# A fused linear-attention and snake-MLP kernel on one core: states of head pairs as one block-diagonal tile, transposes by two routes, a re-planned order of loads and weights, and lent PSUM banks

## The chip, the cores and the metric

One Trainium2 chip, one of its cores. The metric is the device time of one execution in microseconds (us), lower is better. The executions of one kernel mostly lie within one and a half per cent of their median here; those more than 1.5% above the fastest are called slow, and medians below are of fast runs. Each execution also has a *span*, from its first to its last instruction, which lies about 1.7 us under the time of that same execution (250.8 and 252.5 us for the profiled run of the kernel before). Engines: PE multiplies matrices, PEld loads its weights, DVE and POOL do elementwise work, ACT does table functions (exp, ln, sin) and copies, SP issues most of the DMA transfers. PSUM is the memory that PE writes to, used here in eight banks; SBUF is the large on-chip memory. The granted clock is the share of PE's full speed that it was allowed. The DMA share adds up the time of packets, so that it can go above 1.

## The reference, cut to what matters

```python
f = 1 / (1 + exp(-f_logit))                       # batch 4, heads 8, 768 steps, head size 48
for t in range(768):
    state = f[:, :, t, :, None] * state + einsum('bhd,bhe->bhde', k[:, :, t], v[:, :, t])
    y[:, :, t] = einsum('bhd,bhde->bhe', q[:, :, t], state)
x = y as (3072 tokens, 384)
h = x @ w_in                                      # 384 x 2048, "layer one"
g = h + sin(alpha * h)**2 / (alpha + 1e-9)
out = g @ w_out                                   # 2048 x 384, "layer two"
```

## The kernel before

The 768 steps are cut into 6 chunks of 128. Within a chunk, attention is done by matmuls: cumulated logs of the gates (tile cs), gated k and q (tile qk), their transposes (tp in PSUM, tr in SBUF), scores (aps), masked scores (at), output y, and the state (kv in PSUM, st in SBUF) which passes to the next chunk. Four batches make one chunk of 512 tokens (tile xT; in all chunks but the first, six small DMAs, the *spread*, move parts of it to other partitions); then layer one (tile h, 16 tiles of three 512-column matmuls), the sine s, its square, g, and layer two (tile o).

What is special is who decides the order. The kernel contains a small planner. Every operation is put in a list with estimated durations, the engines that may do it and the buffers that it takes; the planner simulates this and fixes one static order for each engine, with a few hand-tuned constants. On the chip each engine runs its list strictly in order.

```python
LAG = 50
ATT = 12
PHASES = [("pre", [0]), ("sin", 1), ("pre", [1, 2]), ("sin", 21), ...]   # ACT's order: exponentials or sines
def in_order(ops, lines):
    ...
            for e, dur in o.engs.items():
                s = max(t, free[e])
                ...
                key = (s + (BIAS[e] if len(o.engs) > 1 else 0), o.rank, s + d)
                if best is None or key < best[0]:
                    best = (key, o, e, s, d)
```

The transposes of chunk 0 are done on PE, those of chunks 1 to 5 by a transposing DMA on SP's queue; the states of two heads are kept as two 64-row halves:

```python
        def tr_(e):
            if e == SP:
                nc.sync.dma_start_transpose(t, qk_b[qkb.place % NQ].rearrange("c x p r e -> c (x p r e)"))
                return
            (nc.scalar.copy if e == ACT else nc.vector.tensor_copy)(t, tl[x, "tp"])
        def inter_(e):
            for p in range(HP):
                for r in range(2):
                    nc.tensor.matmul(y[halves[r], POS[p], :], tl["st", c - 1, b][halves[r], p, :],
                                     tl[x, "tr"][halves[r], HP + p, :], ...)
        ...
    for u in range(2, 2 * NCH):       # loads strictly in the order f, k, q, v of each pair of batches
        for n in "fkqv":
            load(u, n, EARLY + 10 + u)
```

Of the kernel before, what the change touches and what calls it, by code (L numbers as in the profile page):

```python
# [16 lines left out]
N_H, N_A, NQ, NV, NG = 3, 3, 6, 4, 22  # L17
LAG = 50
ATT = 12
PHASES = [("pre", [0]), ("sin", 1), ("pre", [1, 2]), ("sin", 21), ("pre", [3]), ("sin", 4), ("pre", [4]),  # L20
          ("sin", 6), ("pre", [5, 6]), ("sin", 15), ("pre", [7]), ("sin", 15), ("pre", [8, 9]), ("sin",
          6), ("pre", [10, 11]), ("sin", 44)]
RANK = [-100, 26, -206, 68, -82, 12, -28, -12, 36, 24, 32, 16]
MULS = {"POOL": 1180, "DVE": 1000}
BIAS = {"ACT": 300, "DVE": 100, "POOL": -800}
# [22 lines left out]
TABLE_LOAD, DMA_LATENCY, DMA_AHEAD = 1280, 1900, 3000  # L48


def in_order(ops, lines):


    free = dict.fromkeys(("PE", "ACT", "DVE", "POOL", "SP"), 2500)
    free["ACT"] = free["SP"] = 800
    dma_free, table = dict.fromkeys(("SP", "POOL"), 0), None
    follows = {}
    for o in ops:
        for d in set(o.deps):
            follows.setdefault(d, []).append(o)  # L60
    missing = {o: len(set(o.deps)) for o in ops}
    done, turn, nth = [], {o: i for x in lines.values() for i, o in enumerate(x)}, dict.fromkeys(lines, 0)

    def when(o):

        t = max([o.after] + [d.end + (LATENCY[d.eng] if d.eng not in o.engs or len(o.engs) > 1 or d.eng != "PE" else 0)
                             for d in o.deps])
        for b in o.takes:
            if b.place is None:
                i = len(b.ring.taken)  # L70
                if i >= b.ring.n:
                    old = b.ring.taken[i - b.ring.n]
                    if any(x.end is None for x in old.users):
                        return None
                    t = max([t] + [x.end + LATENCY[x.eng] for x in old.users])
        return t

    pending = [o for o in ops if not missing[o]]
    left = len(ops)
    while left:  # L80
        best = None
        for o in pending:
            if o.line and turn[o] != nth[o.line]:
                continue
            t = when(o)
            if t is None:
                continue
            for e, dur in o.engs.items():
                s = max(t, free[e])
                if o.dma:  # L90
                    s = max(s, dma_free[e] - DMA_AHEAD)
                d = dur + (TABLE_LOAD if o.table and o.table != table and table else 0)
# [3 lines that stand above are left out]
        if best is None:  # L96
            raise RuntimeError("no operation can start")
        _, o, e, s, d = best
        o.start, o.eng, free[e] = s, e, s + d
        o.end = s + d  # L100
        if o.dma:
            dma_free[e] = max(s + 600, dma_free[e]) + o.dma
            o.end = dma_free[e] + DMA_LATENCY
        table = o.table or table
        if o.line:
            nth[o.line] += 1
        for b in o.takes:
            if b.place is None:
                b.place = len(b.ring.taken)
                b.ring.taken.append(b)  # L110
        pending.remove(o)
        for x in follows.get(o, ()):
            missing[x] -= 1
            if not missing[x]:
                pending.append(x)
        done.append((o, e))
        left -= 1
    return done
# [3 lines left out]
def kernel(  # L122
# [58 lines left out]
    act_order, load_order, h_order = [], [], []  # L181

    def op(rank, engs, emit, deps=(), takes=(), holds=(), table=None, dma=None):
        o = Op(rank, engs, emit, [d for d in deps if d is not None], list(takes), table, dma)
        for b in list(takes) + list(holds):
# [23 lines left out]
                            pattern=[[-1, C]], channel_multiplier=1)  # L209
    ident_f = consts.tile([FB, FB], F32)  # L210
# [23 lines left out]
    def load(u, n, rank):  # L234
# [7 lines left out]
        o = bufs[n, u].ready = op(rank, {SP: 500}, emit, takes=[bufs[n, u]], dma=2500 if u < 2 else 2200)  # L242
# [11 lines left out]
    def w_in_load(hf, rank):  # L254
        for j, p0, r0, n in ((0, 0, 0, E), (1, 0, 80, E), (2, 16, 3 * D, D), (2, 0, D + 16, 16)):
            for r in range(2):
                def emit(e, j=j, p0=p0, r0=r0, n=n, r=r):
                    nc.gpsimd.dma_start(out=w_in_bf[r * E + p0:r * E + p0 + n, j, HF[hf]],
                                        in_=moe_w_in[4 * D * r + r0:4 * D * r + r0 + n, HF[hf]])
                w_in_dma[hf].append(op(rank, {POOL: 1000}, emit, dma=1300 if n == E else 1000 if n == D else 500))  # L260

    def w_out_load(rank):
        src = moe_w_out.rearrange("(fb p) m -> p fb m", p=P)
        for g4 in range(4):
            def emit(e, gs=slice(4 * g4, 4 * g4 + 4)):
                nc.gpsimd.dma_start(out=w_out_bf[:, gs, :], in_=src[:, gs, :])
            w_out_dma[g4] = op(rank + 0.1 * g4, {POOL: 1000}, emit, dma=3500)

    def alpha(rank):
# [11 lines left out]
        t.after = 6000  # L281
# [5 lines left out]
    def pre(u, rank):  # L287
# [26 lines left out]
        for i in range(2):  # L314
# [23 lines left out]
            def gl_(e, m=m):  # L338
                tl["gl", m] = at_pool.tile([P, HP], F32, tag="gl", bufs=6, name=f"gl_{m}")
                nc.vector.tensor_copy(tl["gl", m], tl["cs", m][:, H * D:H * D + HP])  # L340
# [6 lines left out]
            c_ = op(rank + i, {PE: 170 if last else 420}, cs_, deps=[l], takes=[cb], holds=[lf])  # L347
            gi = op(rank, {ACT: 450}, Gi_, deps=[c_], takes=[Gib], holds=[cb], table=EXP)
# [6 lines left out]
            if not last:  # L355
                made["gl", m] = op(rank + i, {DVE: 100}, gl_, deps=[g], takes=[glb], holds=[cb])
        return act, late

    def pres(us, rank):
        parts = [pre(u, r) for u, r in zip(us, rank)]  # L360
        for a, _ in parts:
            act_order.extend(a)
        for _, l in parts:
            act_order.extend(l)


    def attend(c, b, rank):
# [3 lines left out]
        tpb, trb, ab, atb = first and buf("a"), buf("tr"), [buf("a"), buf("a")], [buf("at0"), buf("at1")]  # L371
# [21 lines left out]
        def a_(e):  # L393
            t = tl[x, "tr"]
            aps = tl[x, "a"] = [ps_a.tile([P, HP, C], F32, tag="a", name=f"aps_{c}_{b}_{r}") for r in range(2)]
# [4 lines left out]
        def m_(e, r):  # L400
            a = tl[x, "at", r] = at_pool.tile([P, HP, C], BF16, tag=f"at{r}", name=f"at_{c}_{b}_{r}")
            nc.vector.tensor_mul(a, tl[x, "a"][r], mask4)  # L402

        def inter_(e):
            y = tl[x, "y"] = ps_a.tile([P, HP, C], F32, tag="a", name=f"y_{c}_{b}")
            for p in range(HP):
                for r in range(2):
                    nc.tensor.matmul(y[halves[r], POS[p], :], tl["st", c - 1, b][halves[r], p, :],
                                     tl[x, "tr"][halves[r], HP + p, :],
                                     start=(p == 0), stop=False, skip_group_check=True)  # L410
# [21 lines left out]
        def kv_(e):  # L432
            kv = tl[x, "kv"] = ps_a.tile([P, HP, E], F32, tag="a", name=f"kv_{c}_{b}")
            if not first:
                nc.tensor.matmul(kv, ident, tl["st", c - 1, b], start=True, stop=False, skip_group_check=True)
            for p in range(HP):
                for r in range(2):
                    nc.tensor.matmul(kv[halves[r], p, :], qk_b[qkb.place % NQ][:, 0, p, r, :], v_b[vb.place % NV][:, i, r, p, :],
                                     start=(first and p == 0), stop=True, skip_group_check=True)

        def st_(e):
            t = tl["st", c, b] = st_pool.tile([P, HP, E], BF16, tag=f"s{b}", name=f"st_{c}_{b}")
            nc.vector.tensor_tensor(t, tl[x, "kv"], tl["gl", m].unsqueeze(2).to_broadcast([P, HP, E]),
                                    Alu.mult)

        if first:
# [3 lines left out]
        else:  # L450
            tr = op(rank, {SP: 1300}, tr_, deps=[made["kh", m], made["qh", m]], takes=[trb], holds=[qkb], dma=1000)
        a = op(rank, {PE: 450}, a_, deps=[tr], takes=ab, holds=[trb])
        ms = [op(rank, {DVE: 690}, lambda e, r=r: m_(e, r), deps=[a], takes=[atb[r]], holds=[ab[r]]) for r in range(2)]
        last_ = None
        if not first:
            last_ = op(rank, {PE: 480}, inter_, deps=[a, made["st", c - 1, b]], takes=[yb], holds=[trb, sold])
# [5 lines left out]
        if not last:  # L462
            kv = op(rank + 1, {PE: 450}, kv_, deps=[made["kh", m], made["v", u], made.get(("st", c - 1, b))],
                    takes=[kvb], holds=[qkb, vb] + ([sold] if sold else []))
            made["st", c, b] = op(rank + 1, {DVE: 420}, st_, deps=[kv, made["gl", m]], takes=[sb], holds=[kvb, bufs["gl", m]])
# [13 lines left out]
    def first(c, fb, ts, rank, needs):  # L479
        n = ts.stop - ts.start  # L480
        half = n < TOK
        hb, sb, s2b = buf("h"), buf("s"), buf("s2")
# [4 lines left out]
        def mm(e):  # L487
            h = tl[x, "h"] = ps_h.tile([P, TOK], F32, tag="h", name=f"h_{c}_{fb}_{ts.start}")
# [24 lines left out]
        a.line = "h"  # L513
        h_order.append(a)
# [5 lines left out]
    def second(c, t, rank):  # L520
        ob, sbuf = buf("o"), buf("osb")
        prev = None
        for fb in range(FB):
# [6 lines left out]
            prev = op(rank + 0.5 * fb, {PE: 163}, mm, deps=[prev, g, w_out_dma[fb // 4]],  # L530
# [9 lines left out]
        op(rank, {SP: 500}, store, deps=[v_], holds=[sbuf], dma=500)  # L540
# [7 lines left out]
    for u in range(2):  # L548
        for n in "fkqv":
            load(u, n, EARLY)  # L550
# [3 lines left out]
    for u in range(2, 2 * NCH):  # L554
        for n in "fkqv":
            load(u, n, EARLY + 10 + u)
# [3 lines left out]
    for what, arg in PHASES:  # L560
        if what == "pre":
            pres(arg, [RANK[u] for u in arg])
            for u in arg:
                c = u // NU
                for b in (2 * (u % NU), 2 * (u % NU) + 1):
                    attend(c, b, base(c) - ATT + 4 * b)
                if u % NU and c:
                    spread(c, base(c) - ATT)
# [13 lines left out]
    for c in range(NCH):  # L582
        for t in range(B):
            second(c, t, base(c) + LAG + 4 * t)
# [3 lines left out]
    for o, e in in_order(ops, {"table": act_order, "load": load_order, "h": h_order}):  # L588
# [34 lines left out]
```

## Time and profile before

| | before |
|---|---|
| time | 254.7 us, median of 3 runs (254.52 to 257.35) |
| span of the profiled run | 250.8 us (that run took 252.5 us) |
| hardware DMA queue (loads, stores, transposes) | 69.3% of 16 engines |

From the page of the kernel before: busy time of each engine with its share of the span, the DMA queue that SP feeds (packets, MB, share of 16 engines), and one of the costlier groups (busy us, mean ns of one | idle time ahead of them, and what ended it):

```profile
PE 198.4 (79%) x1577; PEld 109.8 (44%) x1593; DVE 155.3 (62%) x306; ACT 140.3 (56%) x219; POOL 139.6 (56%) x168
...
q1 hardware_dynamic: 124608, 29.34, 69.3%
...
L398 PE MATMUL aps<-tr 64*128 64x128 bf16 x192 | 12.9, 249 | 7.7 <-DMA tr<-qk 2.6
```

PE is the busiest, but only 79%; the transposing DMAs (tr) hold PE's score matmuls for 2.6 us in all. Next the state's operations, from the groups of all instructions:

```profile
L408 PE MATMUL y<-tr,st 64*64 64x128 bf16 x160 | 9.1, 240 | 0.3 <-DVE st L443 0.3
L438 PE MATMUL kv<-vb,qk 128*64 128x64 bf16 x160 | 7.4, 212 | 1.7 <-POOL qk L343 1.7
L408 PEld LDWEIGHTS <-st 64*64 64x64 bf16 x160 | 5.7, 116 | 5.4 <-issue 4.7 <-DVE qk L343 0.2
L435 PE MATMUL kv<-st,ident 128*128 128x256 bf16 x16 | 4.6, 288 | 1.0 <-DVE qk L343 0.9
L383 PE MATMUL tp<-ident,qk 128*128 128x128 bf16 x32 | 4.1, 309 | 5.4 <-DVE qk L343 3.7 <-POOL qk L343 1.7
L443 DVE TENSOR_TENSOR st<-kv,gl 128x256 bf16<-128x256 f32 x20 | 8.2, 418 | 2.4 <-PE kv L438 2.3
```

The prediction's working rests on these and on the slices, stretches and waits that it shows itself.

### The profile page before, as it was taken

The page shows a single profiled execution, that of the slowest core. Times are in us where ns is not written, and L with a number is a line of the kernel's source. Part 1 is how long each engine was busy: PE and PEld are TensorE (multiplying, and loading weights), DVE is VectorE, ACT ScalarE, POOL GpSimd, SP SyncE. Part 2 cuts the span into 40 slices and gives each one's busy share as a digit, 9 for nine tenths or more (in the row PEclk, how much of TensorE's full clock was granted, in tenths as well). Part 3 has the DMA queues.
Part 4 walks back from the last instruction along what each step waited for, and adds up shares of the span by engine and source line. Part 5 has one row for each costly group of instructions (what it writes and reads, how often), then busy time and mean ns, then how long its engine had stood idle before and what let it go on. Part 6 is the DMA issues. An engine that isn't in the chain of part 4 may idle for free.

```text
span 250.8 us, 4495 instructions
## 1 busy us (share of the span) xinstructions
PE 198.4 (79%) x1577; PEld 109.8 (44%) x1593; DVE 155.3 (62%) x306; ACT 140.3 (56%) x219; POOL 139.6 (56%) x168
## 2 busy tenths in 40 slices
PE   0257107998688594999869999899999899999993
PEld 0145004565355351454434545455444345555552
DVE  3183106776384768497775784597797756666741
ACT  4307129345866487465765558969755454555500
POOL 8653007556342426468444754683758756788810
PEclk9999999999958677699977999999999999999999
DMA  8999999999999996999659802897640001100021
GB/s 140 188 195 207 188 202 187 171 188 196 177 178 183 218 157 107 228 176 189 118 104 191 122 4 66 158 168 169 147 97 5 31 3 68 42 33 34 31 95 63
DMA packets 127798, 32.77 MB, mean 131 GB/s; under 512 B 121392, under 2 KB 127008, under 8 KB 127776
## 3 DMA queue, kind: packets, MB, share of 16 engines
q1 hardware_dynamic: 124608, 29.34, 69.3%
q0 software_dynamic: 3168, 3.16, 8.0%
q8 instruction: 12, 0.20, 0.3%
q14 instruction: 10, 0.08, 0.1%
HBM read 25.17 MB, written 4.72 MB: 119 GB/s over the span
## 4 chain that ended last, share of the span: by engine, by line
PE 35%; POOL 18%; issue 15%; SPq 10%; DMA 9%; DVE 7%; ACT 4%; POOLq 0%; ACTq 0%; DVEq 0%
POOL s L504 16%; PE o L527 16%; PE h L491 14%; SPq L240 9%; DMA f<-in_f_logit_dram 5%; DMA v<-in_v_dram 3%; DVE g L509 2%; PE y L422 2%; POOL qk L343 2%; DVE at L402 2%; PE aps L398 1%; ACT Gi L336 1%; SPq L473 1%; ACT L591 1%; DVE osb L535 1%
## 5 line engine op out<-in xcount | busy, mean ns | idle before, releaser
L504 POOL TENSOR_TENSOR s<-s 128x512 f32<-128x512 f32 (+1 forms) x112 | 102.1, 923 | 58.5 <-ACT s L496 54.1
L496 ACT ACTIVATE s<-h,al_p 128x512 f32<-128x512 f32 (+1 forms) x112 | 68.7, 626 | 60.2 <-PE h L491 54.7
L509 DVE SCALAR_TENSOR_TENSOR g<-s,al_r,h 128x512 bf16<-128x512 f32 (+1 forms) x112 | 74.0, 668 | 30.5 <-POOL s L504 28.8
L491 PE MATMUL h<-xT,w_in_bf 128*128 128x512 bf16 (+1 forms) x320 | 84.6, 374 | 9.1 <-DVE g L509 4.2
L527 PE MATMUL o<-w_out_bf,g 128*128 128x384 bf16 x384 | 82.2, 334 | 0.1
L491 PEld LDWEIGHTS <-w_in_bf 128*128 128x128 bf16 x336 | 33.1, 103 | 37.9 <-issue 12.7
L527 PEld LDWEIGHTS <-g 128*128 128x128 bf16 x384 | 36.7, 99 | 28.2 <-issue 1.1
L343 POOL TENSOR_TENSOR qk<-k,Gi 128x384 bf16<-128x384 f32 x24 | 23.5, 1005 | 39.4 <-ACT Gi L336 39.3
L402 DVE TENSOR_TENSOR at<-aps,mask 128x512 bf16<-128x512 f32 x48 | 31.4, 684 | 8.2 <-PE aps L398 8.0
L323 PE MATMUL cs<-lf,mask 128*128 128x384 bf16 x24 | 8.4, 366 | 14.9 <-ACT lf L296 12.9
L422 PE MATMUL y<-at,vb 128*64 128x128 bf16 x184 | 18.9, 239 | 1.1 <-DVE at L402 0.7
L591 ACT ACT_TABLE_LOAD x15 | 19.2, 1283 | 0.3
L398 PE MATMUL aps<-tr 64*128 64x128 bf16 x192 | 12.9, 249 | 7.7 <-DMA tr<-qk 2.6
L293 ACT ACTIVATE f<-f 128x768 f32<-128x768 f32 x12 | 10.1, 839 | 13.1 <-DMA f<-in_f_logit_dram 13.0
L429 ACT CAST xT<-y 128x512 bf16<-128x512 f32 (+1 forms) x13 | 7.4, 567 | 17.3 <-PE y L422 17.3
L422 PEld LDWEIGHTS <-vb 128*64 128x64 bf16 x184 | 12.3, 119 | 10.3 <-issue 9.3
L340 DVE COPY gl<-cs 128x4 f32<-128x4 f32 x20 | 3.2, 159 | 21.3 <-ACT cs L332 21.3
L535 DVE COPY osb<-o 128x384 f32<-128x384 f32 x19 | 10.5, 556 | 9.0 <-PE o L527 8.7
L343 DVE TENSOR_TENSOR qk<-q,cs 128x384 bf16<-128x384 f32 x24 | 12.9, 546 | 2.9 <-DMA q<-in_q_dram 2.9
L336 ACT ACTIVATE Gi<-cs 128x384 f32<-128x384 f32 x24 | 11.6, 484 | 4.8 <-PE cs L326 4.5
L398 PEld LDWEIGHTS <-tr 64*128 64x128 bf16 x192 | 7.0, 105 | 14.6 <-issue 8.2
L326 PEld LDWEIGHTS <-lf 128*128 128x128 bf16 x80 | 5.0, 102 | 16.3 <-issue 15.1
(48 smaller groups left out, 129.3 us busy)
## 6 DMA issues: line engine op xcount, KB each, us to landing
f<-in_f_logit_dram SPq DMA_DIRECT2D x12, 384.0 KB, 6.5
k<-in_k_dram SPq DMA_DIRECT2D x12, 384.0 KB, 6.2
q<-in_q_dram SPq DMA_DIRECT2D x12, 384.0 KB, 7.2
v<-in_v_dram SPq DMA_DIRECT2D x12, 384.0 KB, 6.7
out_dram<-osb SPq DMA_DIRECT2D x24, 192.0 KB, 2.1
w_out_bf<-in_moe_w_out_dram POOLq DMA_DIRECT2D x4, 384.0 KB, 6.9
w_in_bf<-in_moe_w_in_dram POOLq DMA_DIRECT2D x8, 128.0 KB, 5.8
xT<-xT SPq DMA_DIRECT2D x30, 16.0 KB, 1.8
```

What stands on the lines that cost most here:

```text
L240: engine[e].dma_start(out=t, in_=srcs[n][bp * 2 * H:(bp + 1) * 2 * H, c * C:(c + 1) * C, :] .rearrange("b c d -> c b d"))
L336: nc.scalar.activation(out=tl["Gi", m], in_=tl["cs", m][:, :H * D], func=Act.Exp)
L343: engine[e].tensor_mul(qk_b[bufs["qk", m].place % NQ][:, "kq".index(n), :, :, :D], tl[n, u][:, i * H:(i + 1) * H, :].rearrange("c (r p) d ...
L398: nc.tensor.matmul(aps[r][:, p, :], t[halves[r], p, :], t[halves[r], HP + p, :], start=True, stop=True)
L402: nc.vector.tensor_mul(a, tl[x, "a"][r], mask4)
L422: nc.tensor.matmul(tl[x, "y"][halves[r], blk, :], v_, tl[x, "at", r][:, p, :], start=(first and p == 0), stop=True, skip_group_check=True)
L491: nc.tensor.matmul(h[:, :n], w_in_bf[:, kb, fs], xT[:, kb, ts], start=(kb == 0), stop=(kb == KB - 1))
L496: nc.scalar.activation(out=s[:, :n], in_=tl[x, "h"][:, :n], func=Act.Sin, scale=al_p[:, fb:fb + 1])
L504: engine[e].tensor_mul(s2[:, :n], s[:, :n], s[:, :n])
L509: nc.vector.scalar_tensor_tensor(tl["g", c, fb][:, ts], tl[x, "s2"][:, :n], al_r[:, fb:fb + 1], tl[x, "h"][:, :n], Alu.mult, Alu.add)
L527: nc.tensor.matmul(tl["o", c, t], tl["g", c, fb][:, t * P:(t + 1) * P], w_out_bf[:, fb, :], start=(fb == 0), stop=(fb == FB - 1))
L591: nc.scalar.preload_act_table_set(now)
```

## The change

The intent: fewer and wider state matmuls (a pair of heads as one 128 by 128 block-diagonal tile, half of it zero), fewer transposing DMAs in the stretch where DMA is full, an order of loads, weights and phases fitted to that, and two PSUM banks of layer two lent to layer one while layer two has nothing to do. The diff, cut to its core (left out are other constants of the planner, RANK, BIAS and the DMA latencies among them, which also change the order):

```diff
-N_H, N_A, NQ, NV, NG = 3, 3, 6, 4, 22
-LAG = 50
-ATT = 12
-PHASES = [("pre", [0]), ("sin", 1), ("pre", [1, 2]), ("sin", 21), ...]
+NG = 36
+PE_TR = 4
+SPARE = 25
+LOADS = [("f", 0), ("f", 1), ("k", 0), ("q", 0), ("v", 0), ("q", 1), ("v", 1), ("k", 1), ("f", 2), ...]
+W_AFTER = [15000, 22000, 52000]
+LAG = [50, 24, 32, 29, 28, 94]
+ATT = [-32, 18, 8, 12, -4, 16]
+PHASES = [("pre", [0]), ("pre", [1]), ("sin", 6), ("pre", [2]), ("sin", 16), ("pre", [3]), ("sin", 9), ...]
@@ the planner: weights now also count against SP's queue
+            if e == "POOL":
+                dma_free["SP"] = max(s + 600, dma_free["SP"]) + o.dma
@@ weights are not planned before a given time
+                o.after = W_AFTER[hf]
@@ transposes: chunks 0 to 3 on PE, 4 and 5 by DMA
-        if first:
+        if c < PE_TR:
@@ the state
-                for r in range(2):
-                    nc.tensor.matmul(y[halves[r], POS[p], :], tl["st", c - 1, b][halves[r], p, :],
-                                     tl[x, "tr"][halves[r], HP + p, :], ...)
+                nc.tensor.matmul(y[:, POS[p], :], tl["st", c - 1, b][:, p, :, :].rearrange("d r e -> d (r e)"),
+                                 tl[x, "tr"][:, HP + p, :], ...)
-            t = tl["st", c, b] = st_pool.tile([P, HP, E], BF16, ...)
+            t = tl["st", c, b] = st_pool.tile([P, HP, 2, E], BF16, ...)     # times gl, which is 0 off the diagonal
@@ lent banks
+        spare = c == 0 and nth < SPARE and nth % 5 > 2
-        hb, sb, s2b = buf("h"), buf("s"), buf("s2")
+        hb, sb, s2b = buf("o" if spare else "h"), buf("s"), buf("s2")
```

## The prediction

> **What bounds the kernel now.** I read the slices of the page first, then three long stretches of the span, then the same stretches for layer one alone (tile h), then the list of waits and the chain that ended last.
>
> ```profile
> PE   0257107998688594999869999899999899999993
> PEclk9999999999958677699977999999999999999999
> DMA  8999999999999996999659802897640001100021
> ```
>
> DMA is full for the first half of the span and almost idle in the last quarter; PE is the reverse. So there are two regimes. The stretches size them (columns: length, then busy us and count of PE, PEld, DVE, ACT, POOL; granted clock, DMA share, GB/s), first all work, then layer one alone (PE, DVE, ACT):
>
> ```profile
> 0.00:40.00 40.00, 12.79 (x117) 8.36 (x117) 12.94 (x47) 14.02 (x21) 17.69 (x37) 1.00 1.15 186
> 40.00:100.00 60.00, 46.97 (x435) 29.29 (x436) 41.52 (x95) 40.20 (x69) 29.47 (x43) 0.86 1.22 176
> 100.00:240.00 140.00, 131.56 (x985) 68.23 (x1000) 98.12 (x161) 86.05 (x130) 92.42 (x90) 0.96 0.53 100
> ...
> 0.00:40.00 40.00, 2.88 (x12) 0.48 (x1) 0.47 (x1) 1.00 1.15 186
> 40.00:100.00 60.00, 17.86 (x87) 14.36 (x31) 13.91 (x31) 0.86 1.22 176
> 100.00:240.00 140.00, 63.91 (x222) 58.66 (x80) 54.28 (x80) 0.96 0.53 100
> ```
>
> By 100 us only 99 matmuls of layer one are done: chunk 0 (32 half tiles of 3) and one tile more. All of chunks 1 to 5 and most of layer two lie between 100 and 247 us, with PE 94% busy (131.56 of 140). So the tail is bound by PE, and what set its late start is the first 100 us, where PE waits:
>
> ```profile
> POOL qk L343 <- ACT Gi L336: 39.3, 8, 12.4
> ACT f L293 <- DMA f<-in_f_logit_dram: 13.0, 2, 10.2
> PE cs L323 <- ACT lf L296: 12.9, 3, 10.9
> ...
> 22.84 13.01 DMA f<-in_f_logit_dram
> 35.88 0.85 ACT f L293
> ```
>
> The third load of f (chunk 1) lands only at 35.9 us, and ACT runs its exponentials before those that finish chunk 0's second half. Every engine stands: chunk 0's gates, long computed, wait 12 us behind a load that they don't need. A smaller stop of the same kind is the 6.5 us wait for v at 77 us in the chain.
>
> **What the Trainium skill says.** "DMA: Bandwidth & Descriptors", section "Issuing engines are not separate DMA queues": transfers of all issuers interleave on the same 16 engines. The trace agrees: with weights on POOL's queue from 3.6 us, f takes 13 us from issue to landing against 3.7 for the lone first one. The old plan inside the kernel counted the two queues apart; the new one charges weights to both. "ScalarE: Activation LUTs", "What ACT_TABLE_LOAD costs": about 1283 ns a load; the trace has 15 at 1283 ns. "TensorE: Matmul & The Clock Gate", "HAM oscillation": idle gaps throttle the array; here the granted clock is 0.86 in the stretch with gaps, 0.96 afterwards. "TensorEngine Tiling (Array Packing)", "Key Properties": different tiles can run in parallel. The trace shows little of it for the 64*64 pairs that go: 160 matmuls y<-tr,st took 9.1 us of busy time, 57 ns each, no less than 128 columns at the warm rate below.
>
> **The change part by part.** *PE work before.* In the last, undisturbed part of the chain three h matmuls of 512 columns take 0.65 us, and four o matmuls of 384 columns 0.65 us. That is 0.217 and 0.1625 us each. Layer one: 80 tiles x 3 x 0.217 = 52.0, and 96 half matmuls x 0.108 = 10.4; layer two: 384 x 0.1625 = 62.4. Sum 124.8 us. Attention: between 160 and 206 us PE is busy 42.2 us, holds 67 h and 74 o matmuls (26.5 us), so 15.7 us are some 8 attentions of a batch: 1.96 each, 24 x 1.96 = 47. All in all some 172 us, in a span of 250.8.
>
> *PE transposes for chunks 1 to 3.* 12 batches x 8 = 96 more; the 32 of chunk 0 took 4.1 us busy, 0.128 each: +12.3 us on PE. Their copy out of PSUM is 689 ns on DVE or 1021 on ACT: 12 x 0.69 = 8.3 us of DVE if all are there.
>
> *Block-diagonal states.* The state product y<-tr,st goes from 160 to 80 matmuls at 57 ns: -4.6. kv goes from 160 (7.4 us busy, 46 ns) to 80 of double width at 57: -2.8. The 16 identity matmuls widen from 256 to 512 columns: 256 x 0.217/512 = 0.108 each, +1.7. PE nets +12.3 - 4.6 - 2.8 + 1.7 = +6.6, so 178 us. On DVE the state's product doubles, 418 ns to that of a 128x512 product from PSUM, 684: 20 x 0.27 = +5.3; gl gets some 60 ns x 20 = +1.2. DVE goes from 155.3 to some 170, less what moves to ACT.
>
> *DMA.* While only loads and weights ran the rate was 186 to 197 GB/s; at 190 a 384 KB load is 2.07 us. The software queue (weights) has 8.0% of the span, 20.1 us of share; at the saturated share of 1.22 that is 16.4 us. The hardware queue has 69.3%, 173.8 us; 48 loads are 48 x 2.07 x 1.22 = 121; with some 15 for stores and a few for spreads, each of the 20 transposes is left about 1.8 of share, 1.5 us of a full queue. Twelve removed: 18 us less, all of them in the stretch where DMA is full. They also stand in SP's order, so a transpose that waits no longer holds the loads behind it.
>
> *New order.* f0, f1 come first, weights are held to 15, 22 and 52 us, and chunk 0's second half no longer stands behind f2. With 3 us for the first landing: chunk 0's 8 loads take 16.6 us, some of it shared with weights, so they land at about 23 instead of 30 us. Chunk 1's tensors end at the 19th load, 19 x 2.07 + 3 + 8 for w_in = 50 us, f4 one load later: layer one of chunk 1 can start near 60 us instead of 99. ACT's order then asks for f6 (31st load; 31 x 2.07 + 16.4 + 3 = 84 us) and f9 (37th: 96 us) before it takes the rest of chunk 2. So from about 60 to 100 us it is still the loads that set the pace. From about 100 us nothing waits for DMA.
>
> *Other parts.* 13 table switches instead of 15: 2 x 1.28 on ACT, off the path. g goes from 22 to 36 buffers, which lets layer one run ahead before w_out comes. The two spare PSUM banks help chunk 0 alone: its h tiles turn over in 5 banks rather than 3, a few us at most, hidden behind chunk 1's loads. Squares shift from POOL (1044 ns each, now all 112) towards ACT and DVE by the weaker bias.
>
> *Sum.* By 100 us PE should have done chunk 0 (20.8 for the layers + 8 attention), chunk 1 (20.8 + 8.5), of chunk 2 three tiles (2) + 8.5 and chunk 3's attention (8.5): 77 us. There remain 178 - 77 = 101. At the 94% busy that the same mix reached before, 101/0.94 = 108 us, so the last matmul ends near 208. Before, that was at 247.0 with the span ending 3.8 later: span 212. Time is 254.7 against a span of 250.8, so 3.9 more: 216 us.
>
> **The rivals.** *(1) DVE and ACT become the bound between 60 and 130 us.* A chunk's attention with transposes is on DVE 8 masks x 0.684 + 4 q x 0.546 + v 2.1 + 4 states x 0.69 + gl 0.9 = 13.5 us, plus 16 adds x 0.744 = 11.9; transposes' copies, xT and output copies add up to 8 more. That is 25 to 33 us, against PE's 29. For it: DVE was already 70% busy after 100 us. Against it: ACT (140 of 250 us) can take the copies. If so, 225 to 232. *(2) The clock holds and PE keeps 98%*, as between 140 and 160 us before (19.71 of 20): 101/0.98 saves 5 us: 211; with loads at 2.0 us some 207. *(3) SP's order goes wrong again*: a store or spread waits at the head of the queue and holds loads; SP waited some 48 us for output copies in front of stores before, most of it late. A stop of 10 us gives 226. *(4) No gain*, because PE is the bound and gets 6.6 us more: it would need the first 100 us to stay as empty as they are; the wait on f at 22.8 us is plainly one of order, so I give it little.
>
> **Range and chances.** The sum says 216; rivals 1 and 3 are likelier than 2, which makes the upper side longer: 207 to 231. Even at its end the gain is 9%. Faster by over 2%: 0.95; within: 0.035; slower: 0.015.
>
> **What would show it.** PE busy should be 195 to 205 us in a span near 212, so its share above 90% against 79. Layer one by 100 us should count some 150 matmuls, not 99. ACT's wait for f around 23 us should be gone, qk on POOL behind Gi fall from 39.3 us to under 20; shorter waits on f near 55 and 85 to 95 us should remain. DMA should run dry by 130 us apart from eight transposes and stores. tp should be 128 matmuls. The prediction is wrong if PE's idle time after 100 us goes over 15 us, if DVE passes 90% in the middle, or if the loads take much over 2.1 us each.

## The result, and the profile after

The changed kernel takes 233.5 us (median of four fast runs, 232.77 to 234.23), the kernel before in the same rounds 255.78. The ratio is 0.9126, with a 95% interval of 0.9052 to 0.92. Ratios here are the mean time of one kernel's fast runs over that of the other's fast runs in the same rounds, so not quite the ratio of the medians. The gain is 8.7%: the direction was right, the size was not. Predicted were 216.0 us, with a range to 231.

The same parts of the page for the changed kernel:

```profile
PE 193.7 (83%) x1529; PEld 111.8 (48%) x1529; DVE 167.4 (72%) x319; ACT 149.0 (64%) x239; POOL 121.2 (52%) x148
...
PE   0441587787769999987999999999979999799993
...
PEclk9999999799999999999999999999999999999999
DMA  7999999986890799973999944700049101010011
...
q1 hardware_dynamic: 111936, 26.19, 55.8%
```

PE is now 90% busy or more in 23 of the 28 slices from the thirteenth on (5.8 us each), the clock is granted nearly in full, and DMA has holes already before 100 us. The stretches that the prediction used (length; busy us and count of PE, PEld, DVE, ACT, POOL; clock, DMA share, GB/s), all work:

```profile
0.00:40.00 40.00, 18.80 (x173) 13.65 (x173) 20.30 (x61) 19.14 (x30) 15.86 (x37) 1.00 1.09 200
40.00:100.00 60.00, 52.20 (x476) 32.90 (x476) 50.28 (x100) 45.89 (x81) 36.77 (x45) 0.97 0.89 155
100.00:240.00 140.00, 122.75 (x883) 65.20 (x883) 96.84 (x158) 84.00 (x130) 68.55 (x67) 0.99 0.38 88
```

and layer one alone (PE, DVE, ACT):

```profile
0.00:40.00 40.00, 5.73 (x33) 2.51 (x6) 2.64 (x6) 1.00 1.09 200
40.00:100.00 60.00, 21.48 (x108) 20.96 (x39) 20.57 (x41) 0.97 0.89 155
```

By 100 us 33 + 108 = 141 matmuls of layer one are done, against 99 before. After 100 us PE has 122.75 us of work left, against 138.6 (131.56, and 7.1 after 240 us): 15.9 us of the 18.4 by which the span became shorter. The waits of the changed kernel that answer to those of before (us in total, times, longest):

```profile
POOL qk L358 <- ACT Gi L349: 27.1, 7, 4.5
...
ACT f L306 <- DMA f<-in_f_logit_dram: 2.4, 1, 2.4
```

The 10 us wait of ACT for the third f is gone; ACT waits for f only once, for 2.4 us, at the very start. So where did the rest of the expected gain go? ACT's timeline shows how late layer one begins (start, duration, what):

```profile
29.03 1.28 ACT L606 ACT_TABLE_LOAD   x1
30.33 1.33 ACT L514 ACTIVATE s<-h,al_p 128x256 f32<-128x256 f32 x3
...
68.86 1.28 ACT L606 ACT_TABLE_LOAD   x1
...
77.69 1.28 ACT L606 ACT_TABLE_LOAD   x1
78.98 1.63 ACT L514 ACTIVATE s<-h,al_p 128x256 f32<-128x256 f32 x3
```

Each table load is a switch between exponentials and sines. The first sines of chunk 0 run at 30.3 us, and the first of chunk 1 only at 79 us, where the prediction had chunk 1's layer one "near 60 us". Between 69 and 78 us ACT does nothing but exponentials and gates (and one copy), one after another, with hardly a gap. But ACT is not the only gate. The last copy of chunk 1's attention into xT starts at 72.3 us; SP then issues the spread, and PE's first matmuls of chunk 1's layer one follow it (SP, then PE):

```profile
73.04 3.76 SPq L488 DMA_DIRECT2D xT<-xT  x6
...
77.42 0.38 PE L509 MATMUL h<-xT,w_in_bf 128*128 128x512 bf16 x1
78.03 1.25 PE L509 MATMUL h<-xT,w_in_bf 128*128 128x512 bf16 x5 [0.23 <-DMA xT<-xT]
```

So both ways end near 77.5 us: chunk 1's attention and spread on the one side, ACT's order on the other.

### The profile page after: what moved, and what is told of

It is laid out like the page before. It is cut to its first block, busy times and chain, and to the rows that moved or that the text cites. A ratio compares the mean times of both kernels' runs of the same rounds, so it can differ in the third digit from the quotient of the medians.

```text
span 232.4 us, 4292 instructions
## 1 busy us (share of the span) xinstructions
PE 193.7 (83%) x1529; PEld 111.8 (48%) x1529; DVE 167.4 (72%) x319; ACT 149.0 (64%) x239; POOL 121.2 (52%) x148
## 3 DMA queue, kind: packets, MB, share of 16 engines
q1 hardware_dynamic: 111936, 26.19, 55.8%
## 4 chain that ended last, share of the span: by engine, by line
PE 49%; DVE 13%; DMA 13%; SPq 7%; POOL 6%; issue 5%; ACT 5%; POOLq 0%; ACTq 0%
PE h L509 19%; PE o L546 18%; DMA v<-in_v_dram 6%; PE y L437 6%; DVE g L527 5%; SPq L488 4%; SPq L251 4%; POOL s L522 3%; DVE at L419 3%; DMA w_out_bf<-in_moe_w_out_dram 3%; DMA xT<-xT 2%; POOL qk L358 2%; PE aps L416 2%; DMA w_in_bf<-in_moe_w_in_dram 2%; ACT Gi L349 1%
## 5 line engine op out<-in xcount | busy, mean ns | idle before, releaser
L522 POOL TENSOR_TENSOR s<-s 128x512 f32<-128x512 f32 (+1 forms) x94 | 87.8, 944 | 63.5 <-ACT s L514 51.3
L527 DVE SCALAR_TENSOR_TENSOR g<-s,al_r,h 128x512 bf16<-128x512 f32 (+1 forms) x112 | 72.4, 664 | 19.1 <-POOL s L522 18.4
L509 PE MATMUL h<-xT,w_in_bf 128*128 128x512 bf16 (+1 forms) x336 | 78.5, 355 | 6.8 <-DMA xT<-xT 3.6
L546 PE MATMUL o<-w_out_bf,g 128*128 128x384 bf16 x384 | 78.5, 327 | 2.8 <-DMA w_out_bf<-in_moe_w_out_dram 1.9
L546 PEld LDWEIGHTS <-g 128*128 128x128 bf16 x384 | 34.4, 97 | 27.6 <-issue 3.1
L358 POOL TENSOR_TENSOR qk<-k,Gi 128x384 bf16<-128x384 f32 x19 | 19.0, 1017 | 33.8 <-ACT Gi L349 27.1
L606 ACT ACT_TABLE_LOAD x13 | 16.7, 1283 | 0.2
L458 DVE TENSOR_TENSOR st<-kv,gl 128x512 bf16<-128x512 f32 x20 | 13.7, 685 | 4.0 <-PE kv L452 4.0
L416 PE MATMUL aps<-tr 64*128 64x128 bf16 x192 | 10.8, 225 | 6.3 <-DVE qk L358 5.6
L399 PE MATMUL tp<-ident,qk 128*128 128x128 bf16 x128 | 11.5, 236 | 4.4 <-DVE al_p L290 2.4
L349 ACT ACTIVATE Gi<-cs 128x384 f32<-128x384 f32 x24 | 11.7, 486 | 4.2 <-PE cs L336 2.7
L554 DVE COPY osb<-o 128x384 f32<-128x384 f32 x14 | 7.7, 555 | 7.7 <-PE o L546 6.7
L399 PEld LDWEIGHTS <-qk 128*128 128x128 bf16 x128 | 9.2, 106 | 6.7 <-POOL qk L358 4.2
L416 PEld LDWEIGHTS <-tr 64*128 64x128 bf16 x192 | 6.0, 96 | 12.4 <-DVE qk L358 6.6
```

What stands on the lines that cost most here:

```text
L349: nc.scalar.activation(out=tl["Gi", m], in_=tl["cs", m][:, :H * D], func=Act.Exp)
L358: engine[e].tensor_mul(qk_b[bufs["qk", m].place % NQ][:, "kq".index(n), :, :, :D], tl[n, u][:, i * H:(i + 1) * H, :].rearrange("c (r p) d ...
L399: nc.tensor.transpose(tl[x, "tp"][:, j * HP + p, :], qk_b[qkb.place % NQ][:, j, p, :, :].rearrange("c r e -> c (r e)"), ident)
L416: nc.tensor.matmul(aps[r][:, p, :], t[halves[r], p, :], t[halves[r], HP + p, :], start=True, stop=True)
L509: nc.tensor.matmul(h[:, :n], w_in_bf[:, kb, fs], xT[:, kb, ts], start=(kb == 0), stop=(kb == KB - 1))
L522: engine[e].tensor_mul(s2[:, :n], s[:, :n], s[:, :n])
```

## The experiments

Eighteen kernels ran, each timed in three rounds beside the kernel before (whose medians over all runs were 254.5 to 256.2 us). They ran in five groups on three chips; the changed kernel itself was run again in the first group only, so that most differences below are across groups. The yardstick below is 233.9 us, the median of the changed kernel's seven fast runs in two groups; differences under some 2 us are not resolved. The edits are to the changed kernel.

My first theory was that loads stop on SP's queue behind other work (A: two stops of about 12 us at 47 and 61 us), so that a deeper pool of load buffers and loads issued earlier give back most of the missing 17 us. The rivals: ACT's or DVE's own work sets the pace up to 100 us (B), and PE stands for the weights of layer two (C).

### The changed kernel again

> The changed kernel once more, as the measure for the others of this group: 233 to 235 us, ratio to the kernel before 0.905 to 0.92.

Measured: 233.92 us over its three fast runs, ratio 0.9222 (0.9046 to 0.9397); the fourth was slow. It repeats.

### Loads set free (theory A)

```diff
-    ld = pool("ld", 3)
+    ld = pool("ld", 5)
+    ahead = [x for x in plan[at:] if x[0].line == "load"][:8]        # at: chunk 1's spread
+    plan = plan[:at] + ahead + [x for x in plan[at:] if x not in ahead]
```

> The changed kernel with 5 instead of 3 buffers for each loaded tensor, and with the eight loads that stand behind chunk 1's spread put in front of it; everything else in the same order. Theory A (loads that stand still on SP's queue, 12 us behind a buffer of k and 12 us behind the spread, make the middle late): 8 to 15 us less than the changed kernel. Theory B (DVE and ACT are the bound from 37 to 60 us) and theory C (PE stands for w_out from 62 to 66 us): within 2 us of it, though DMA is busy where it was idle.

Measured: 237.03 us, ratio 0.9353: 3 us slower. Two stretches of this kernel:

```profile
40.00:60.00 20.00, 15.04 (x160) 11.23 (x161) 17.35 (x39) 17.31 (x33) 12.95 (x19) 0.91 1.15 203
60.00:80.00 20.00, 15.61 (x145) 9.78 (x142) 14.54 (x31) 14.99 (x28) 9.95 (x14) 0.99 1.07 189
```

and the same of the changed kernel:

```profile
40.00:60.00 20.00, 14.98 (x160) 11.14 (x160) 17.33 (x39) 17.39 (x33) 12.92 (x19) 0.91 0.90 154
60.00:80.00 20.00, 17.29 (x163) 11.06 (x162) 14.82 (x32) 15.58 (x30) 9.85 (x14) 1.00 0.62 106
```

The DMA share went from 0.90 and 0.62 to 1.15 and 1.07: the loads did come earlier. The work of DVE and ACT in these stretches did not change. But the edit has a price of its own: in the busier queue chunk 1's spread lands later, PE waits 2.8 us for xT between 70 and 90 us (0.2 in the changed kernel), and layer one of chunk 1 begins at 79.1 instead of 77.4. That can account for most of the 3 us lost. A gain of the size that theory A expected, 8 to 15 us, isn't there; that earlier loads are worth nothing, this run alone doesn't show. The kernel with long rows, below, has no such price.

### Weights of layer two earlier (theory C)

```diff
+    early = [x for x in plan if x[0] in w_out_dma.values()]      # moved to what is planned for 38 us
```

> The changed kernel with the four loads of w_out issued ahead of what is planned for 38 us, instead of from 53 us on; everything else in the same order. Theory C: PE's stop for w_out goes and 3 to 5 us with it. Theories A and B: within 1.5 us, or a little slower where the weights delay chunk 1's loads.

Measured: 235.09 us, ratio 0.9287. No gain. PE's wait for these weights, 1.9 us, is gone, but ACT's third stretch of exponentials began at 54.9 instead of 52.0 us: POOL spent 3.1 us, from 41.9 us on, issuing the weights ahead of two gated k, PE's transposes waited 2.6 us for these, and ACT 3.1 us for PE. By 69 us the lag was down to 0.8 us. A wait was exchanged for another, so C isn't cleanly tested; the wait that it names is too short for much of the missing 17 us.

### Loads from long rows

The same bytes, from rows of 3072 instead of 192 bytes. The values are wrong (relative error 1.4).

```diff
-            engine[e].dma_start(out=t, in_=srcs[n][...].rearrange("b c d -> c b d"))
+            engine[e].dma_start(out=t.rearrange("c b d -> c (b d)"), in_=flat[n][u])
```

> The changed kernel with each load taken from a contiguous block (rows of 3072 bytes instead of 192), in the same order: wrong values on purpose, the same bytes, much faster loads. The prediction's premise (loads set the pace up to 100 us): 12 us faster or more. Theory B (PSUM banks of layer one, ACT and DVE bound the stretch from 29 to 80 us): only the first 25 us of loading shrink, 3 to 8 us faster.

Measured: 231.64 us, ratio 0.9095: some 2 us at most. The queue's line:

```profile
q1 hardware_dynamic: 19776, 26.19, 34.9%
```

55.8% of 232.4 us is 129.7 us; 34.9% of 230.5 is 80.4. Some 49 us of DMA time were taken out, and 2 of time came back. This settles one thing: in the changed kernel the loads are not what sets the pace from 60 to 100 us. And an early start alone isn't enough either. The switches to the first sines of chunk 0 and of chunk 1 in this kernel:

```profile
23.16 1.28 ACT L607 ACT_TABLE_LOAD   x1
...
75.92 1.28 ACT L607 ACT_TABLE_LOAD   x1
```

In the changed kernel they were at 29.03 and 77.69: of a lead of 5.9 us, 1.8 were left.

### Extra work on one engine at a time (theory B)

If one engine bounded a stretch, doubling one of its operations there would cost its full duration, and work added elsewhere nothing.

```diff
-            nc.vector.tensor_mul(tl[x, "at", r], tl[x, "a"][r], mask4)
+            for _ in range(2 if c == 1 else 1):                       # and c == 3 in another kernel
+                nc.vector.tensor_mul(tl[x, "at", r], tl[x, "a"][r], mask4)
```

Masks of chunk 1 twice (8 x 0.684 = 5.5 us on DVE):

> The changed kernel with the eight mask products of chunk 1 done twice: 8 x 0.68 = 5.5 us more of DVE between 40 and 72 us, same result. Theory B: 4 to 6 us slower. Theories A and C: at most 1.5 us slower, since DVE's added work lies in waits for loads or w_out.

Measured: 238.5 us, +4.6. Masks of chunk 3 twice:

> The eight mask products of chunk 3 done twice, 5.5 us more of DVE between 100 and 135 us, where the prediction called PE the bound. If PE alone bounds the later part: at most 2 us slower. If DVE bounds there too, as chunk 1's doubled masks (4 us slower) suggest for the early part: 4 to 6 us slower.

Measured: 237.69 us, +3.8.

```diff
-            nc.scalar.activation(out=s[:, :n], ..., func=Act.Sin, ...)
+            for _ in range(2 if c == 0 and ts.start else 1):
+                nc.scalar.activation(out=s[:, :n], ..., func=Act.Sin, ...)
```

Sines of chunk 0's second half twice (ACT's busy time rose by 7.0 us, from 149.0 to 156.0):

> The changed kernel with the 16 sines of chunk 0's second half done twice: 16 x 0.42 = 6.7 us more of ACT between 41 and 69 us. Theory B, ACT in that stretch on the path: 5 to 8 us slower. Were ACT's waits there for loads, or for PE alone, the added work would lie in them: at most 2 us slower.

Measured: 237.59 us, +3.7. Score matmuls of chunk 3 three times:

```diff
-                    nc.tensor.matmul(aps[r][:, p, :], ...)
+                    for _ in range(3 if c == 3 else 1):
+                        nc.tensor.matmul(aps[r][:, p, :], ...)
```

> The score matmuls of chunk 3 done three times: 64 more matmuls at 0.056 to 0.08 us, 3.6 to 5 us more of PE between 100 and 135 us, same result. If PE bounds the later part: 3 to 5 us slower. If DVE or ACT does: at most 2 us.

Measured: 235.71 us, +1.8; PE's busy time rose by 3.0 us.

So 5.5 us on DVE cost 4.6 and 3.8, 7 on ACT cost 3.7; the 1.8 for 3 us on PE isn't resolved. On DVE and ACT nothing is free. If one engine alone were the bound, work on another would cost nothing, so no single engine bounds the kernel; after 100 us too, where PE is over 92% busy, DVE's work still counts. What the test can't tell apart: a doubled operation fills its engine, and it also makes the chain that it stands in longer.

### Squares of chunk 0 left out

The reverse of the last group: h, its sine, its square and the sum form a chain that holds a PSUM bank, so a shorter chain would turn the banks over faster. The values are wrong (relative error 0.41).

```diff
+            if c == 0:
+                tl[x, "s2"] = s
+                return
```

> The changed kernel without the squares of chunk 0's layer one (the add reads the sine itself): wrong values on purpose, the same order. It takes 0.6 us out of the chain that holds a PSUM bank of h, and 18 us off POOL, ACT and DVE between 29 and 69 us. Theory B: 4 to 8 us faster. If chunk 0's layer one is hidden behind loads or other work, as the prediction had it: within 2 us.

Measured: 235.61 us, ratio 0.9234: no gain. The chain that holds the banks does not bound chunk 0. Why a kernel with less work isn't even a little faster I can't show; its granted clock was lower between 40 and 80 us (0.83 and 0.91 in the two stretches of 20 us, against 0.91 and 1.00).

### The parts of the change undone

The order of every engine is kept in the first three. Transposes of chunks 1 to 3 back on DMA:

```diff
         def tp_(e, j):
+            if c:
+                return
...
-            if e == SP:
+            if c:
```

> The changed kernel with the transposes of chunks 1 to 3 given back to DMA, in the same order of everything else. The prediction's premise (loads set the pace up to 100 us, each DMA transpose takes 1.5 us of a full queue and holds SP's order): 10 to 18 us slower than the changed kernel. Theory B (DVE and ACT bound the stretch from 37 to 80 us): they lose 13.6 us of copies and PE 12 us of transposes, so within 3 us either way, unless SP's order stops the loads.

Measured: 243.29 us, ratio 0.9514: +9.4. A wait of this kernel between 40 and 100 us:

```profile
PE aps L418 <- DMA tr<-qk: 7.7, 3, 5.1
```

The scores stand for transposes that sit in the full DMA queue. The loads behind them suffer too: DVE waits 4.0 us for v between 40 and 100 us, in three waits, where the changed kernel has none. (The order was made for transposes on PE; a plan made for these might lose less.) States as two halves again:

```diff
-                nc.tensor.matmul(y[:, POS[p], :], tl["st", c - 1, b][:, p, :, :].rearrange("d r e -> d (r e)"), ...)
+                for r in range(2):
+                    nc.tensor.matmul(y[halves[r], POS[p], :], tl["st", c - 1, b][halves[r], p, :], ...)
...                                                                    # and kv, st, gl as before the change
```

> The changed kernel with the states as before (two 64x64 matmuls a pair, states of 256 columns), in the same order. Theory B: DVE is rid of 5.3 us, a quarter of it in the stretch that binds: 1 to 2 us faster. The prediction's premise (PE is the bound and block-diagonal states spare it 5.7 us): 3 to 6 us slower.

Measured: 234.92 us, ratio 0.9217: no difference that the runs resolve. The rows show why. State operations with halves in this kernel:

```profile
L458 DVE TENSOR_TENSOR st<-kv,gl 128x256 bf16<-128x256 f32 x20 | 8.4, 419 | 4.8 <-PE kv L453 4.8
L423 PE MATMUL y<-tr,st 64*64 64x128 bf16 x160 | 8.2, 222 | 0.0
L453 PE MATMUL kv<-vb,qk 128*64 128x64 bf16 x160 | 6.7, 210 | 0.8 <-DVE st L458 0.5 <-ACT tr L405 0.3
L450 PE MATMUL kv<-st,ident 128*128 128x256 bf16 x16 | 4.8, 303 | 0.0
```

and block-diagonal in the changed kernel (with its transposes, tp, for the account below):

```profile
L458 DVE TENSOR_TENSOR st<-kv,gl 128x512 bf16<-128x512 f32 x20 | 13.7, 685 | 4.0 <-PE kv L452 4.0
...
L399 PE MATMUL tp<-ident,qk 128*128 128x128 bf16 x128 | 11.5, 236 | 4.4 <-DVE al_p L290 2.4 <-POOL qk L358 1.4 <-DVE qk L358 0.6
...
L452 PE MATMUL kv<-vb,qk 128*128 128x128 bf16 x80 | 8.1, 227 | 1.1 <-DVE st L458 0.8 <-ACT tr L407 0.3
...
L424 PE MATMUL y<-tr,st 128*128 128x128 bf16 x80 | 7.8, 219 | 0.0
...
L450 PE MATMUL kv<-st,ident 128*128 128x512 bf16 x16 | 6.1, 380 | 0.3 <-DVE qk L358 0.3
...
L424 PEld LDWEIGHTS <-st 128*128 128x128 bf16 x80 | 5.8, 98 | 3.5 <-PE cs L339 0.2
```

On PE 8.2 + 6.7 + 4.8 = 19.7 us became 7.8 + 8.1 + 6.1 = 22.0. Half as many matmuls are no less work: 80 full ones take 98 ns each, as much as two halves at 51 ns (8.2 us for 160). One weight load of a full one also takes 98 ns. One of a half took 116 ns in the kernel before, yet 160 of them fit in 5.7 us, so the loads of halves overlap. That the weight load sets the pace of the full ones is my reading; no run tests it. Both undone:

> Both of these undone at once: what is left of the change is the new order of loads, weights and operations, the buffers and the PSUM banks lent. If the order is where the gain comes from: at most 4 us slower than the changed kernel, so 18 us faster than before. If the transposes and states carry it: 10 us slower or more.

Measured: 249.58 us over all four runs, 247.4 over the two fast ones (245.97 and 248.84), ratio 0.9697 (0.9554 to 0.984). So the new order, buffers and weights alone give about 8 of the 22 us. With DMA transposes the block-diagonal states seem to be worth some 4 us (247.4 to 243.3), but the intervals of the two ratios overlap (0.9554 to 0.984, 0.9402 to 0.9627), so this isn't resolved; with PE transposes they are worth nothing that shows.

The lent banks were tried with another setting, which makes the planner work out another order:

```diff
-SPARE = 25
+SPARE = 0        # and 32 in another kernel
```

> The changed kernel without PSUM banks lent to layer one in chunk 0 (the order is worked out anew). The prediction called the banks a few us at most, hidden behind loads: within 2 us. Theory B: chunk 0's layer one is in the stretch that binds, and a bank of h is held from the matmul to the add on DVE: 2 to 5 us slower.

Measured: 245.61 us, +11.7. Lending to all 32 half tiles:

> PSUM banks lent to all 32 half tiles of chunk 0 instead of the first 25, order worked out anew. If the banks themselves are worth the 11 us that were lost without them: within 3 us of the changed kernel, or a little faster. If any step away from the tuned setting spoils the order that is worked out (which would take the loss without banks out of the argument): 6 us slower or more.

Measured: 241.5 us, +7.6. More banks and fewer banks both cost much. A tuned order that was lost can explain both, but isn't shown: with 32 lent, layer two also has to wait for a later tile (in the code it starts after the last lent one). What the banks are worth by themselves stays open: with the order kept, fewer lent banks deadlocked when built, and so didn't run. The kernel before with PE transposes in its own plan doesn't build either: its planner finds no operation that can start.

### The first 30 us

DVE's timeline in the changed kernel (in brackets the idle time ahead, and what ended it) shows a stop that the planner didn't foresee:

```profile
18.68 0.55 DVE L358 TENSOR_TENSOR qk<-q,cs 128x384 bf16<-128x384 f32 x1 [4.00 <-DMA q<-in_q_dram]
...
22.87 0.36 DVE L315 CAST vb<-v 128x384 bf16<-128x384 f32 x1 [2.50 <-DMA v<-in_v_dram]
...
23.66 1.28 DVE L419 TENSOR_TENSOR at<-aps,mask 128x512 bf16<-128x512 f32 x2
```

In DVE's fixed order q and v of chunk 0's second half stand ahead of the masks of its first half. Both loads are late, because POOL issues the weights of layer one beside them from 9.2 us, where the plan had 15:

```profile
9.16 4.27 POOL L269 DMA_DIRECT2D w_in_bf<-in_moe_w_in_dram  x8
```

Three kernels act on this. First, the two casts of v go from DVE to POOL:

```diff
-            nc.vector.tensor_copy(vo[:, :, 0:2, :D], vi[:, :, 0:2, :])
-            nc.vector.tensor_copy(vo[:, :, 2:4, 16:], vi[:, :, 2:4, :])
+            nc.gpsimd.tensor_copy(vo[:, :, 0:2, :D], vi[:, :, 0:2, :])
+            nc.gpsimd.tensor_copy(vo[:, :, 2:4, 16:], vi[:, :, 2:4, :])
```

> The changed kernel with the two casts of v for each load on POOL instead of DVE, in the same order: 12 to 13 us less of DVE, as much or more on POOL, which was 52% busy. Theory B: added DVE work cost 0.7 of itself, so 3 to 7 us faster, less what POOL's waits for v cost. If DVE isn't on the path: within 1.5 us.

Measured: 230.2 us over its three fast runs (229.01 to 230.51; the slow one 232.68), ratio 0.901 (0.8938 to 0.9082): 3.7 us faster, and correct. Second, the weights are held by a one-column copy on POOL that reads the second q:

```diff
+                    if hf == 0 and j == 0 and r == 0:
+                        nc.gpsimd.tensor_copy(held, tl["q", 1][:, 0, 0:1])
```

> The changed kernel with w_in really held until the load of q for chunk 0's second half has landed (about 15 us), by one small copy on POOL that reads that load; the order is the same. In the changed kernel the loads of w_in went out at 9 us, where its plan has 15. Theory D (the order is right, and its first slip of 4 us, from early weights, is carried to the end): 2 to 5 us faster. Theory B alone: within 1.5 us, since the first sine only moves within idle time.

Measured: 233.77 us, ratio 0.9169: nothing. Its switch to the first sines came at 23.75 instead of 29.03 us, but that to chunk 1's sines at 77.1 against 77.7: the head start was gone by then. Third, the casts moved for chunks 0 and 1 alone:

```diff
+            (nc.gpsimd if u < 4 else nc.vector).tensor_copy(vo[...], vi[...])
```

> v's two casts go from DVE to POOL for the tensors of chunks 0 and 1 alone (4 of 12 tensors). If the relief of DVE counts only before 100 us, where PE is not yet the bound, this gives all of the 3.5 us that moving all twelve gave: 229.5 to 231. If what counts is DVE's work anywhere, as the doubled masks of chunk 1 and of chunk 3 (which cost nearly the same) let one expect, it gives a third of it: 232 to 233.5.

Measured: 229.6 us over its three fast runs (228.2 to 231.35; the slow one 232.96), ratio 0.9034. Four of the twelve tensors give the whole gain, as far as the runs resolve it, so it comes from the first chunks and not from DVE's load in general. What happened is more than a relief of DVE. POOL's timeline in this kernel:

```profile
12.11 0.51 POOL L315 CAST vb<-v 128x384 bf16<-128x384 f32 x1 [2.17 <-DMA v<-in_v_dram]
...
13.00 2.65 POOL L269 DMA_DIRECT2D w_in_bf<-in_moe_w_in_dram  x5
```

The cast waits for v, and the weights stand behind it: they are issued from 13.0 us instead of 9.2. And DVE's first masks in this kernel:

```profile
16.73 1.28 DVE L419 TENSOR_TENSOR at<-aps,mask 128x512 bf16<-128x512 f32 x2
```

7 us earlier. This start is kept: the switch to chunk 1's sines comes at 72.8 us, against 77.7. Last, both together:

> All twelve v casts on POOL, and the first weights held on POOL until q of the second load has landed. The hold alone made the first sine 5 us earlier and gained nothing in the end. If that start was lost to DVE's order, then with DVE relieved it should be kept in part: 226 to 229. If it is lost to the rest of the order whatever DVE does, the time is that of the casts alone, 229.5 to 231.5. This is also the version meant to beat both kernels.

Measured: 232.56 us, ratio 0.9172: 3.0 us slower than the casts of chunks 0 and 1 alone in the same group (229.6). Its weights start at 15.7 us, and the lead is lost again: chunk 1's sines come at 76.0. So the moment of the weights counts beside DVE's relief: with the casts moved, 13.0 us did better than 15.7. How much each of the two is worth no run separates; none has the weights at 13 us with the casts on DVE. With the hold alone, PE's weight loads stood 2.1 us for w_in between 20 and 80 us, 1.4 in the kernel of chunks 0 and 1, 0.4 in the changed kernel. That is too little to account for the whole loss of 5 us, and the rest of it stays open.

The kernels with v's casts on POOL alone, at 230.2 and 229.6 us, beat both the kernel before and the changed one.

## Why the prediction was wrong in size

**The bound of the kernel before** was read rightly: its late start, not PE, was the thing to win. The wait on f at 22.8 us went as foretold, and 8.7% came out.

**The step that failed** is the one marked *Sum*: "By 100 us PE should have done chunk 0 ..., chunk 1 ..., of chunk 2 three tiles ... and chunk 3's attention (8.5): 77 us." In the same units, the changed kernel had done 96 half matmuls (10.4) and 45 full ones (45 x 0.217 = 9.8) of layer one, 76 matmuls of layer two (76 x 0.1625 = 12.4), and 11 batches of attention (8 for chunk 0, 7 x 2.1 for the rest: 22.7). That is 55 us, not 77. Of the 22 missing, 2.6 are of layer one (153 matmuls expected, 141 found), 8.5 of layer two (128 and 76), and the rest of attention (16 batches and 11).

**The rest of the sum came out, in part by luck.** 178 - 55 = 123 us should have remained, and the trace has 122.75 after 100 us. But the 178 us rest on two errors that cancel: transposes were put 4.9 us too high (12.3 for 7.4), and the states 6.6 too low (5.7 less, where 21.1 us of the kernel before became 22.0). At 94% the 123 us take 131, which puts the last matmul at 231 and the span at 234 or 235; the last matmul ended at 228.9, with PE 95% busy, and the span was 232.4. Last, 3.9 us were added for the time, from 254.7 less 250.8. These are of different executions: the profiled one took 252.5, so 1.7 was right (a span lies about 1.7 us under the time of that same execution), and the prediction would have been 213.7, further off.

**The premise beneath the sum** was "from about 60 to 100 us it is still the loads that set the pace". The runs contradict it: loads with 49 us less of DMA time gave 2 us, and ACT waited for f only once. What failed is the term "layer one of chunk 1 can start near 60 us". The loads were as computed: chunk 1's last, the 19th, was issued by 42.2 us, and with the median of 5.8 us from issue to landing of all loads it was there near 48 (an estimate; 50 was said). Layer one of chunk 1 began at 77.4 us on PE, 79 on ACT. Between lie ACT's exponentials for chunk 1's second half, which its order puts after the sines of chunk 0 (53.3 us), the attention (last copy into xT at 72.3), and the spread (73.0 to 77), for which the sum has no term. I counted when data lands and took it that work starts then. Chunk 0 began late too, at 29 us, although its last loads had landed at 22.9 (v) and 24.4 us (k); but this alone isn't the cause: with the start at 23.2 (long rows) and 23.8 (weights held) the time fell by 2.3 and 0.2 us. Moving v's casts of chunks 0 and 1 gave some 4 us, so that much of the lateness comes from DVE's order and the moment of the weights' issue together. The rest I only argue: between 40 and 60 us DVE and ACT are 87% busy each, so a list in fixed order has little room to catch up, and added work on either cost 0.5 to 0.8 of itself.

**The size of the parts.** Block-diagonal states were to save PE 4.6 + 2.8 - 1.7 = 5.7 us; they cost 2.3 against halves in the same order. I had seen 57 ns for each half, about what 128 of 512 columns at 0.217 us make (54), and put the same for a full one; that took 98 ns. The cost on DVE was right (+5.3: 8.4 to 13.7), that of gl was not there (159 ns before, 161 after). PE transposes were to cost PE 12.3 us; 128 of them take 11.5 where 32 took 4.1, so 7.4. Taking them from DMA was worth 9.4 us of time, through PE's waits for the transposed tiles (7.7 us between 40 and 100 us with them back) and through DVE's for the loads behind them (4.0). The table loads went from 15 to 13, 1283 ns each, as foretold. The reading of the clock proved less than it said: 0.86 from 40 to 100 us, but 1.00 in the first 40 us, where PE stood most (busy 12.79 us of 40).

**The rivals.** The first, "DVE and ACT become the bound between 60 and 130 us ... 225 to 232", came nearest, and its sign appeared: DVE is 91% busy from 80 to 100 us (18.13 of 20). But neither of the two is the bound alone, and the stretch that counts begins earlier. The third, SP's order, is in the trace with two stops of 12 us, and loads set free of them gained nothing. The range was too narrow upwards because it gave the pace of the first 100 us no doubt of its own.

**Signs that I named.** PE's busy time was 193.7 (195 to 205 said), its share 83% and not above 90; POOL's wait for Gi is 27.1, not under 20; the waits for f near 55 and 90 us did not come, which was the plainest sign that the loads weren't the pace. PE's idle time after 100 us was 9.7 us, under the 15 set as a limit.

## What to carry to other kernels

When several engines run fixed orders with little slack, a list of landing times gives only a bound for the start of work: walk each engine's order and ask what stands ahead of the first useful instruction. Before counting on fewer and fuller matmuls, take the duration of a full one from the trace, not that of the half. And test a tuned order by adding a few us to one engine at a time: where everything costs a part of itself, no single relief will give its whole.

## What the Trainium skill lacked or had wrong

- "Advanced Engine Details and Errata", section "X-Bar Transpose (TRN2)", says that transposing DMAs are as fast as regular ones, and gives 350 to 400 GB/s as the rate to expect. The first half agrees with the changed kernel: from 175 to 178 us, where only transposes are under way, the queue moved 207, 182 and 192 GB/s, and the loads from 85 to 99 us made 211. The rate to expect was not reached; SP took 1.29 us to issue each transpose of 262 KB, which alone holds a row of them to 204 GB/s (an estimate from that duration). And twelve more of them in a busy queue (151.3 us of share, 62.4% of 242.4, against 129.7) made scores wait 10.0 us in four waits, the longest 5.1 us.
- "DMA: Bandwidth & Descriptors", section "Why small descriptors are slow (HBM only)", names 27% overhead at 256 bytes, and by its formula 3 cycles on 6, a third of the time, at 192 (an estimate from the page); it names a second cost, of descriptor data, without a time. With rows of 3072 bytes the whole queue gave up 49.3 of its 129.7 us of share, 38%, although it also holds stores, spreads and transposes, so the loads gave up more than a third. What both costs make together is lacking.
- No page that I read says what a wait of one engine is worth in a kernel whose engines run fixed orders: here 5.5 us more on DVE cost 4.6 and 3.8, 49 us less DMA gained 2, and moving the casts of four tensors gained some 4.
